# A fused attention and two-MoE kernel on one core: late weights loaded into tiles of other owners, and a re-ordered last stage

## The chip, the cores and the metric

The kernel runs on one core of one Trainium2 chip. The metric is the device time of one execution in microseconds (us), lower is better. The engines are PE (matrix products; PEld is its weight load), DVE (vector), ACT (scalar functions and copies), POOL (a second, slower vector engine) and SP, which here only issues DMAs from HBM.

## The reference

Three blocks follow each other. All inputs are float32 except the last three weight matrices, which come out of the third block's draw in float64.

```
B, H, S, D = 4, 8, 576, 64; stride = 32
scores = q @ k.T / sqrt(D)              # heads 0-3: rel in [0, 32); heads 4-7: pos equal modulo 32, causal
attn   = softmax(mask(scores)) @ v      -> x: 2304 x 512
logits = x @ phi                        # 512 x 32: 8 experts of 4 slots
slots  = softmax(logits, over tokens).T @ x          # 32 x 512
for e in 8: slot_out[e] = relu(slots[e] @ w1[e]) @ w2[e]    # 512 x 1024, 1024 x 512
x      = softmax(logits, over slots) @ slot_out
out    = (silu(x @ w_gate) * (x @ w_val)) @ w_out    # 512 x 1536 twice, 1536 x 512
```

## The kernel before, in words

**Attention stage.** Sixteen units (two batches times one head each) run in a software pipeline that one loop counts by `n`. Iteration `n` multiplies unit `n`'s queries and keys (L283) on PE, adds the mask and takes the maximum on DVE (L287, L288), transposes unit `n-1` (L300), takes exponentials on ACT (L293), and multiplies unit `n-1` by its values (L316). Keys lie in three tiles `k0` to `k2`, values in two tiles `v0` and `v1`, the masks in `ml` and `ms`; all of these lie in the pool `ld`. POOL copies each value tile once more into its lower 32 partitions (L261). Between the units stand the transposes of finished heads (L335, copied out by ACT at L337), the logits (L357) and, at the end, the softmax over tokens and the slots (L378 to L473). Lists called `side`, `mid_`, `late` and `first_` say behind which part of which iteration such a step is put.

**Expert stage.** `w1_mm` (L631) runs over the 16 halves of w1 in the order `W1ORDER`, then L722 over the 16 halves of w2 in the order `W2ORDER`. Each half is a tile of 128x2048 (1 MB), loaded as two DMAs of 512 KB.

**Loads.** SP issues every load in the order of the program text, and a load waits on SP until its tile is free; whatever stands behind it on SP waits too. `load_half` takes the next entry of a list. Fifteen weight tiles lie in pool `wp`. Before, the weights 22, 24 and 26 go to a pool `wp2` that takes the place of `ld` after the last unit, and halves of the weights 0, 13, 14 and 15 go into tiles of the attention stage (`wx`, `tmp`).

**Last stage.** The 2304 tokens form blocks `bi` of 512, 512, 512, 512 and 256; the 1536 hidden columns form 12 slices `f`. A step (`bi`, `f`) is `gv` (two products, L800 and L801, then Silu on ACT, a product on DVE, a rounded copy `hh` on ACT and the rest `hl` on POOL, L806 to L809) and, three steps (`LAG`) later, `omm` (L827: 12 products of 128x512 for a block of 512). `CUTS` says which slices of a block are summed in which of three passes; after a pass the block's four PSUM banks are evacuated by DVE and ACT (L852, L858, L862). A slice `f` can be used when its float64 weights have been turned into float32: per 1 MB tile two magnitudes on ACT (`mag`, L199), two clamps on POOL (L206), and three operations each on both halves on DVE (`shift`, `low`, `sign`: L217, L221, L225). For a gate/value tile `g` two small products follow (`a_mm` L780, `a_st` L787) that give `St`. `ORDER` is the order of these tiles, `stage` starts one, `part` issues one DVE operation when a budget (`room`) allows it. `HEAD` is the order of the first small steps; `warm` issues products with no use but to keep PE busy.

Of the kernel before, what the change touches and what calls it, by code (L numbers as in the profile page):

```python
# [32 lines left out]
WORDER = PRE[:2] + list(range(1, 13)) + list(W2ORDER[:6]) + list(SPEC) + [SPLIT] + list(W2ORDER[6:6]) + PRE[2:] + list(W2ORDER[6:])  # L33
# [3 lines left out]
ORDER = [("g", 2), ("g", 3), ("o", 1), ("g", 4), ("o", 2), ("g", 5), ("o", 3), ("g", 6), ("g", 7), ("g", 8), ("g", 9), ("o", 4), ("g", 10), ("g", 11), ("o", 5)]  # L37
LAG = 3
CVC = 0.6
CLP = "go"  # L40
WTAIL = 4
NQK = 3
# [7 lines left out]
ROOM0 = 0.1  # L50
STG = 2
ROOMS = (0.8, 1.2, 0.6)
ROOM = 2.5
EV = 1.1
DIRECT = (2,3,2)
# [58 lines left out]
def build(ctx: ExitStack, tc: tile.TileContext, cst, phi, kq, vh, w1, w2, wgv, wo, out):  # L114
# [9 lines left out]
    pp = [es_p.enter_context(tc.tile_pool(name="pp", bufs=1, space=bass.MemoryType.PSUM))]  # L124
    es_ld = ExitStack()
    lp = es_ld.enter_context(tc.tile_pool(name="ld", bufs=1, side="right"))
    es_att = ExitStack()
# [17 lines left out]
    for j in range(NV):  # L145
        vt.append(lp.tile([96, 2 * NT * (HD + 1)], F32, name=f"v{j}"))
    col = lp.tile([128, 128], F32, name="col")
    par = lp.tile([128, 16], F32, name="par")
    loc = lp.tile([128, 8], F32, name="loc")
    ml = lp.tile([128, 5, 96], BF16, name="ml")  # L150
    ms = lp.tile([128, 9, 96], BF16, name="ms")

    wsrc = [w1[j] for j in range(16)] + [w2[j] for j in range(16)]
    loads = [(j, hf) for j in WORDER for hf in range(2)]
    loads.remove((SPLIT, 0))
    loads.remove((SPEC[0], 1))
    loads.insert(2 * (NB + 2 + NB2), (SPLIT, 0))
    loads.insert(2 * (NB + 2), (SPEC[0], 1))
    wt, gt = {}, {}
    wn = [0]  # L160
    NW = len(loads)

    def load_half(k, pool=wp, bufs=NB):
        for _ in range(k):
            if wn[0] >= NW:
                return
            j, hf = loads[wn[0]]
            if j in SPEC:
                wt[j, hf] = (ap_.tile([128, 1024], F32, tag="wy" if hf else "xT", name="wx", bufs=1) if j == SPEC[0] else
                             ap_.tile([128, 1024], F32, tag="x", name="wx", bufs=6))  # L170
            elif j == SPLIT:
                wt[j, hf] = ap_.tile([128, 1024], F32, tag="eT", name="wx", bufs=1) if hf else tmp[:, 0:1024]
            elif hf == 0:
                a = pool.tile([128, 2048], F32, tag="w", name="w", bufs=bufs)
                if j in PRE:
                    gt[j] = a.bitcast(I32)
                wt[j, 0], wt[j, 1] = a[:, 0:1024], a[:, 1024:2048]
# [271 lines left out]
    def weights_b():  # L449
# [12 lines left out]
    szt = []  # L462

    szp = []

    def slot_in(st, bp):
# [4 lines left out]
        if bp:  # L471
            for y in range(2):
                DVE.tensor_copy(szt[0][:, 2 * y + st, :].rearrange("p (e k) -> p e k", k=36)[:, :, 0:4],  # L473
                                szp[0][:, 64 * st + 32 * y:64 * st + 32 * y + 32].rearrange("p (e j) -> p e j", j=4))
# [9 lines left out]
    with tc.manual_schedule():  # L484
# [39 lines left out]

        def strided():
            for i in range(NT):
# [7 lines left out]
        POOL.memset(eT, 0.0)  # L534

# [23 lines left out]
        for bp in range(2):  # L559
# [5 lines left out]
            else:  # L565
                for fn, d in ((tok_max, 1), (tok_nm, 1), (e_perm, 2), (tok_end, 2), (tok_copy, 2)):
                    at_late(b0 + d, fn, 0)
# [10 lines left out]
            else:  # L578
                at_late(b0, load_half, 4)
                at_late(b0 + 1, warm, WTAIL)  # L580
                for fn, *a in ((etr, 1, 0), (etr, 1, 1), (slot, 1, 0, 0, 3), (etr, 1, 2),
                               (slot, 1, 0, 3, 9), (load_half, 2), (slot_end, 1, 0), (slot, 1, 1, 0, 9),
                               (slot_end, 1, 1), (slot_in, 0, 0), (slot_in, 1, 0), (slot_in, 0, 1),
                               (load_half, 2), (warm, WT[0]), (slot_in, 1, 1), (warm, WT[1])):
                    at_late(b0 + 2, fn, *a)
        at_late(0, strided)
        at_late(1, sels)
        for k, n in PRECONV:
            at_late(k, pre, n)
        n = 0  # L590
        while n < 16 or any(k >= n for k in late):
# [15 lines left out]
            if 0 <= n - 1 < 16:  # L607
                pv(n - 1)
                load_v(n + 1)
                if n == 16:  # L610
                    load_half(2 * (NB + 2) + 1 - wn[0])
                    es_ld.close()
                    wp2 = es_w2.enter_context(tc.tile_pool(name="wp2", bufs=NB2, side="right",
                                                           reuse_waits="tile"))
                    load_half(2 * NB2, wp2, NB2)
                    szt.append(wp2.tile([128, 4, 288], F32, name="sz", bufs=1))
                    POOL.memset(szt[0], 0.0)
# [146 lines left out]
        acc = [fr.tile([128, 512], F32, name=f"acc{t}") for t in range(18)]  # L764

# [118 lines left out]
        def stage(n):  # L884
            if queue and len(staged) < 2:
# [112 lines left out]
```

## Time and profile before

| what | us |
|---|---|
| runs | 346.71, 348.81, 349.77 (median 348.81) |
| profiled execution, its own time | 347.91 |
| its span, first to last instruction | 346.1 |
| PE busy | 330.6 (96%) |
| DVE, ACT, POOL busy | 223.6, 192.7, 139.6 |
| DMA moved | 71.93 MB, mean 208 GB/s |

The span splits into the attention stage (0 to 105.2 us), the expert stage (105.2 to 139.9) and the last stage (from 145.2, the first L800). "Idle before" in square brackets is time in which the engine had nothing running just before that row, and what released it. Times are counted from the span's start.

### The profile page before, as it was taken

How to read it: one execution, taken by the hardware profiler on the slowest of the kernel's cores; microseconds unless marked ns; L12 is line 12 of the kernel's file. 1: busy time of each engine (PE TensorE's matmuls, PEld its weight loads, DVE VectorE, ACT ScalarE, POOL GpSimd, SP SyncE). 2: the span in 40 equal slices, each digit the busy share in tenths (PEclk: the TensorE clock that was granted, in tenths of full speed). 3: DMA queues.
4: the chain of work that ended last, by engine and by line, in shares of the span. 5: the costliest groups of instructions: out<-in, count | busy, mean ns of one | idle time of the engine just before them, and what ended most of it. 6: DMA issues, size and time to landing. Idle time of an engine off the chain costs nothing.

```text
span 346.1 us, 7436 instructions
## 1 busy us (share of the span) xinstructions
PE 330.6 (96%) x2852; PEld 246.5 (71%) x2852; DVE 223.6 (65%) x472; ACT 192.7 (56%) x460; POOL 139.6 (40%) x169
## 2 busy tenths in 40 slices
PE   8799999899999999989996999999999999999995
PEld 5588888697774433567774777777776888888884
DVE  5998888878550356477879588978886233243342
ACT  3798898886530123567567455655556344354441
POOL 2232333112300200357546549655857543443431
PEclk9999999999999999999999899999999999999999
DMA  7999999997899999823335506333000002030331
GB/s 284 411 409 407 396 400 390 407 407 270 280 377 335 411 411 399 321 101 123 128 116 151 205 16 236 122 124 121 1 2 0 0 18 105 0 121 2 123 121 61
DMA packets 20803, 71.93 MB, mean 208 GB/s; under 512 B 2336, under 2 KB 2720, under 8 KB 20768
## 3 DMA queue, kind: packets, MB, share of 16 engines
q1 hardware_dynamic: 20624, 71.45, 55.0%
q8 instruction: 22, 0.36, 0.4%
q14 instruction: 13, 0.11, 0.1%
q10 hardware_dynamic: 144, 0.01, 0.0%
HBM read 66.73 MB, written 4.72 MB: 206 GB/s over the span
## 4 chain that ended last, share of the span: by engine, by line
PE 70%; DVE 12%; DMA 8%; ACT 6%; issue 2%; POOL 1%; SPq 0%; DVEq 0%; POOLq 0%
PE o L827 35%; DMA w<-in_w 5%; PE pv L722 4%; PE sc L631 4%; PE sc L283 4%; PE pv L316 3%; PE gv L800 3%; DMA v<-in_vh 3%; PE gv L801 3%; DVE h L807 3%; PE tr L300 2%; PE tr L335 2%; DVE cv L217 2%; ACT tmp L293 1%; PE tr L482 1%
## 5 line engine op out<-in xcount | busy, mean ns | idle before, releaser
L809 POOL TENSOR_TENSOR hl<-h,hh 128x512 fp32r<-128x512 f32 (+1 forms) x60 | 72.6, 1210 | 88.5 <-ACT hh L808 88.4
L827 PE MATMUL o<-woh,hh 128*128 128x512 f32 (+1 forms) x222 | 86.8, 392 | 2.1 <-DVE acc L852 1.6
L827 PE MATMUL o<-wol,hh 128*128 128x512 f32 (+1 forms) x222 | 86.1, 390 | 0.0
L807 DVE TENSOR_TENSOR h<-gv,sg 128x512 f32<-128x512 f32 (+1 forms) x59 | 37.5, 636 | 60.9 <-ACT sg L806 48.8
L827 PE MATMUL o<-woh,hl 128*128 128x512 f32 (+1 forms) x222 | 66.2, 391 | 0.0
L808 ACT CAST hh<-h 128x512 fp32r<-128x512 f32 (+1 forms) x60 | 34.7, 578 | 52.0 <-DVE h L807 51.0
L827 PEld LDWEIGHTS o<-woh,hh 128*128 128x128 f32 x222 | 41.9, 189 | 13.4 <-DVE acc L852 2.8
L261 POOL COPY v<-v 32x390 f32<-32x390 f32 (+1 forms) x48 | 23.7, 528 | 61.9 <-DMA v<-in_vh 54.8
L827 PEld LDWEIGHTS o<-woh,hl 128*128 128x128 f32 x222 | 42.0, 191 | 9.2
L827 PEld LDWEIGHTS o<-wol,hh 128*128 128x128 f32 x222 | 42.0, 189 | 8.4
L806 ACT ACTIVATE sg<-gv 128x512 f32<-128x512 f32 (+1 forms) x60 | 33.4, 557 | 23.8 <-PE gv L800 23.3
L293 ACT ACTIVATE tmp<-tmp,mx 128x96 f32<-128x96 f32 x144 | 40.1, 368 | 9.3 <-DVE mx L288 9.3
L283 PE MATMUL sc<-k 64*64 64x96 f32 x576 | 27.7, 246 | 1.4 <-DVE tmp L287 1.1
L800 PE MATMUL gv<-cs,St 128*128 128x512 f32 (+1 forms) x60 | 25.4, 423 | 2.3 <-DVE St L789 2.0
L283 PEld LDWEIGHTS sc<-k 64*64 64x64 f32 x576 | 24.3, 133 | 4.4 <-DVE tmp L287 1.7
L771 POOL TENSOR_TENSOR wol<-wo,woh 128x512 fp32r<-128x512 f32 x12 | 15.3, 1288 | 23.8 <-ACT woh L768 23.8
L316 PEld LDWEIGHTS pv<-v,tmp 96*64 96x64 f32 x576 | 19.8, 137 | 6.1 <-ACT tmp L301 5.0
L301 ACT COPY tmp<-tr 96x384 f32<-96x384 f32 x48 | 19.6, 477 | 7.8 <-PE tr L300 7.7
L316 PE MATMUL pv<-v,tmp 96*64 96x65 f32 x576 | 22.3, 226 | 1.4 <-ACT tmp L301 1.1
L801 PE MATMUL gv<-cs,St 128*128 128x512 f32 (+1 forms) x59 | 22.3, 377 | 0.5 <-DVE h L807 0.4
L300 PE MATMUL tr<-cst_t,tmp 128*96 128x128 f32 x144 | 20.0, 280 | 1.5 <-ACT xT L337 1.5
L221 DVE SCALAR_TENSOR_TENSOR cv<-g,cv 128x512 int32<-128x512 int32 x30 | 20.8, 694 | 0.8
(161 smaller groups left out, 460.3 us busy)
## 6 DMA issues: line engine op xcount, KB each, us to landing
w<-in_w SPq DMA_DIRECT2D x56, 512.0 KB, 8.1
g<-in_wgv SPq DMA_DIRECT2D x10, 1024.0 KB, 5.0
k<-in_kq SPq DMA_DIRECT2D x16, 576.0 KB, 7.7
g<-in_wo SPq DMA_DIRECT2D x5, 1024.0 KB, 4.9
v<-in_vh SPq DMA_DIRECT2D x16, 292.5 KB, 6.2
out<-osb SPq DMA_DIRECT2D x17, 256.0 KB, 2.1
wx<-in_w SPq DMA_DIRECT2D x7, 512.0 KB, 5.3
w<-in_wgv SPq DMA_DIRECT2D x4, 512.0 KB, 7.8
```

The source lines that it names most:

```text
L261: POOL.tensor_copy(t4[0:W - 64, :, i0:i1, :], t4[64:W, :, i0 - 1:i1 - 1, :])
L283: PE.matmul(out=ps[h, W * (i - i0):W * (i - i0) + W], lhsT=q[h, 64 * i:64 * i + 64], rhs=k[h, c0:c0 + W], start=True, stop=True, skip_grou ...
L293: ACT.activation(out=e[:, i], in_=e[:, i], func=AF.Exp, scale=1.0, bias=mx[:, i:i + 1])
L300: PE.transpose(ps[0:W, 128 * j:128 * j + 128], e[:, 3 * t + j], ident)
L316: PE.matmul(out=ps[64 * b:64 * b + 64, 65 * (i - i0):65 * (i - i0) + 65], lhsT=attile[0:W, i, 64 * b:64 * b + 64], rhs=v[0:W, 65 * (NT * b ...
L800: PE.matmul(out=pg[:, 0:n], lhsT=St[f][:, 0:128], rhs=csf[:, t0:t0 + n], start=True, stop=True)
L801: PE.matmul(out=pvv[:, 0:n], lhsT=St[f][:, 128:256], rhs=csf[:, t0:t0 + n], start=True, stop=True)
L806: ACT.activation(out=sg[:, 0:n], in_=pg[:, 0:n], func=AF.Silu)
L807: DVE.tensor_tensor(out=h[:, 0:n], in0=pvv[:, 0:n], in1=sg[:, 0:n], op=ALU.mult)
L808: ACT.copy(hh[bi, f][:, 0:n], h[:, 0:n])
L809: POOL.tensor_tensor(out=hl[bi, f][:, 0:n], in0=h[:, 0:n], in1=hh[bi, f][:, 0:n].bitcast(F32), op=ALU.subtract)
L827: PE.matmul(out=o[:, 0:c], lhsT=(a, a, l)[i][:, 128 * t:128 * t + 128], rhs=(woh, wol, woh)[i][f][:, c * k:c * k + c], start=(first and i ...
```

## The change

1. **Homes.** The pools `wp2` and the closing of `ld` are gone. `HOME` names, half tile by half tile, a tile that the attention stage has finished with: key and value tiles, the mask tile, `tmp`, `eT`, `xT` and the six `x` tiles. `LOADS` is a written list of all loads, and `WSCHED` and some `at_step`/`at_late` say when each is issued. `W1ORDER` changes so that the weights in attention tiles (`ATT`) are used by the eleventh place.
2. **Masks.** All masks lie in one tile `mt`. Six of the nine strided masks are computed before the first unit, three after it. The clearing of `eT` on POOL moves from the start to iteration 3.
3. **Copies.** The three copies L337 of one head pair (1,0,0) go from ACT to DVE; in iteration 11 they come ahead of the other late steps, and the copy `Lb` ahead of `e_perm`. One `warm` product less at the end of the attention stage (`WTAIL`).
4. **Last stage.** `CUTS`: block 0's second pass has slices 1 to 3 (was 1 to 4), block 4's has slice 3 alone (was 3 to 5). `ORDER` converts g5 and g6 ahead of o2. `STG` 1 (was 2), `ROOM` 2.4 (was 2.5). `HEAD` puts a transpose (`t`) ahead of `a0` and both `s` steps ahead of the `warm` products. The order of the first eight `acc` tiles and the `g` buffers in memory changes.
5. **Clamps.** `DC=(0,0,2)` files the two clamps of a staged tile under step `n+0`, whose list has already been run when `stage(n)` files them. The built program has no clamp on POOL at all (29 before). The clamps matter only for weights outside float32's range.

```diff
-NB2 = 3
-SPEC = (0, 14, 15)
-SPLIT = 13
-WORDER = PRE[:2] + list(range(1, 13)) + list(W2ORDER[:6]) + list(SPEC) + [SPLIT] + ...
+HOME = {(0, 1): "wy", (0, 0): "xT", (11, 0): "tmp1", (13, 0): "tmp0", (13, 1): "eT",
+        (14, 0): "x", (14, 1): "x", (15, 0): "x", (15, 1): "x", (12, 0): "x", (12, 1): "x",
+        (26, 0): "k1", (26, 1): "k2", (28, 0): "k0", (28, 1): "mt", (11, 1): "v0", (30, 0): "v1"}
+LOADS = (both(*PRE[:2], *range(1, 11), 16, 18, 20, 22) + [(26, 0), (26, 1)] + both(24) +
+         [(0, 1), (28, 0), (28, 1), (11, 1), (13, 0), (30, 0), (0, 0), (11, 0)] + both(14, 15) +
+         [(13, 1), (12, 0), (12, 1)] + both(PRE[2]) + [(30, 1)] + both(*range(17, 32, 2)))
-W1ORDER = (1, 2, 3, 4, 5, 6, 0, 7, 14, 8, 15, 9, 10, 13, 12, 11)
+W1ORDER = (1, 2, 3, 4, 0, 14, 5, 15, 6, 13, 12, 11, 8, 10, 7, 9)
-ORDER = [("g", 2), ("g", 3), ("o", 1), ("g", 4), ("o", 2), ("g", 5), ("o", 3), ("g", 6), ("g", 7), ("g", 8), ...
+ORDER = [('g', 2), ('g', 3), ('o', 1), ('g', 4), ('g', 5), ('g', 6), ('o', 2), ('g', 7), ('o', 3), ('g', 9), ...
+MSC = 6
+TC = 2
+FST = (11,)
+ETM = 3
+DC = (0, 0, 2)
+XTD = {(1,1,1):(0,1),(1,0,0):(0,1,2)}
-WTAIL = 4
+WTAIL = 3
-STG = 2
+STG = 1
-ROOM = 2.5
+ROOM = 2.4
-HEAD = "h g a0 t a1 t s0 w1 s1 p1 w1"
+HEAD = 'h g t a0 a1 t s0 s1 w1 p1 w1 w1'
-WHEAD = 5
-WSCHED = [2]*12+[4,4,2,0,0]
+WHEAD = 4
+WSCHED = [2]*12+[2,2,2,2,0]
-CUTS = [(0, 1, 5, 12), (0, 2, 6, 12), (0, 2, 7, 12), (0, 3, 8, 12), (0, 3, 6, 12)]
+CUTS = ((0, 1, 4, 12), (0, 2, 6, 12), (0, 2, 7, 12), (0, 3, 8, 12), (0, 3, 4, 12))
...
-        cp_ = DVE.tensor_copy if (bp, y, st) == (1, 1, 1) and t in (0, 1) else ACT.copy
+        cp_ = DVE.tensor_copy if t in XTD.get((bp, y, st), ()) else ACT.copy
...
+        strided(0, MSC)
+        at_late(0, strided, MSC, NT)
+        at_late(ETM, POOL.memset, eT, 0.0)
+        at_step(13, load_half, 1)
+        at_late(14, load_half, 3)
+        at_step(15, load_half, 3)
+        at_late(15, load_half, 1)
...
-                    load_half(2 * (NB + 2) + 1 - wn[0])
-                    es_ld.close()
-                    wp2 = es_w2.enter_context(tc.tile_pool(name="wp2", bufs=NB2, side="right", ...
-                    load_half(2 * NB2, wp2, NB2)
+                    load_half(2)
...
-            for fn, a in late.pop(n, []) + first_.pop(n, []):
+            last_, f_ = late.pop(n, []), first_.pop(n, [])
+            for fn, a in f_ + last_ if n in FST else last_ + f_:
...
-                        at(n + 1 + k, fn, k)
-                staged.append((n + 2, kind, j, parts[z:]))
+                        at(n + DC[k], fn, k)
+                staged.append((n + DC[2], kind, j, parts[z:]))
```

**SP at the end of the attention stage.** `w` is a weight tile of `wp` (or, before, of `wp2`), `wx` a weight in an attention tile. Before:

```order
L258 DMA v1_80<-in_vh 64x1170
L182 DMA w_1354<-in_w2 128x1024 x2
L258 DMA v0_79<-in_vh 64x1170
L258 DMA v1_80<-in_vh 64x1170
L182 DMA wx_1676<-in_w1 128x1024
L182 DMA w_1682<-in_w2 128x1024 x2
L182 DMA w_1685<-in_w2 128x1024 x2
L182 DMA w_1688<-in_w2 128x1024 x2
L182 DMA tmp_86<-in_w1 128x1024
```

Now:

```order
L204 DMA w_1345<-in_w2 128x1024 x2
L204 DMA w_1393<-in_w2 128x1024
L280 DMA v0_79<-in_vh 64x1170
L204 DMA w_1393<-in_w2 128x1024
L204 DMA k1_77<-in_w2 128x1024
L280 DMA v1_80<-in_vh 64x1170
L204 DMA k2_78<-in_w2 128x1024
L204 DMA w_1555<-in_w2 128x1024 x2
L204 DMA wx_1603<-in_w1 128x1024
L204 DMA k0_76<-in_w2 128x1024
L204 DMA mt_81<-in_w2 128x1024
```

The value loads of the last units no longer stand behind the pair that waits for the second preloaded tile's conversion (w_1354, now w_1555), and the loads into key, mask and value tiles stand between and behind them.

**ACT at the start of the last stage**, from the second step's Silu (`sg`) to the first evacuation. Before:

```order
L806 ACTIVATE sg_2294<-gv_2290 128x512
L808 CAST hh_2296<-h_2295 128x512
L806 ACTIVATE sg_2315<-gv_2311 128x512
L808 CAST hh_2317<-h_2316 128x512
L199 ACTIVATE wg3_2168<-g_2172 128x512 x2
L852 COPY acc2_2216<-o_2332 128x512
```

Now:

```order
L827 ACTIVATE sg_2284<-gv_2280 128x512
L829 CAST hh_2286<-h_2285 128x512
L221 ACTIVATE wg3_2157<-g_2169 128x512 x2
L827 ACTIVATE sg_2306<-gv_2302 128x512
L829 CAST hh_2308<-h_2307 128x512
L873 COPY acc2_2161<-o_2321 128x512
```

The two magnitudes stand ahead of the third step's Silu instead of behind its `hh`.

**DVE where block 4's first pass ends** (`acc16` evacuates its bank; `h` is a step's product). Before:

```order
L807 TENSOR_TENSOR h_2660<-gv_2656,sg_2659 128x512
L225 SCALAR_TENSOR_TENSOR wo0_60<-g_2360,cv_2643 128x512
L217 TENSOR_SCALAR cv_2668<-wo0_60 128x512
L221 SCALAR_TENSOR_TENSOR cv_2668<-g_2360,cv_2668 128x512
L852 COPY acc16_2230<-o_2619 128x512
L807 TENSOR_TENSOR h_2692<-gv_2688,sg_2691 128x512
L225 SCALAR_TENSOR_TENSOR wo0_60<-g_2360,cv_2668 128x512
L217 TENSOR_SCALAR cv_2705<-wg1_59 128x512
L221 SCALAR_TENSOR_TENSOR cv_2705<-g_2438,cv_2705 128x512
L225 SCALAR_TENSOR_TENSOR wg1_59<-g_2438,cv_2705 128x512
L789 TENSOR_TENSOR St4_2182<-gv_2727,St4_2182 64x256
```

Now:

```order
L828 TENSOR_TENSOR h_2650<-gv_2646,sg_2649 128x512
L243 SCALAR_TENSOR_TENSOR cv_2630<-g_2348,cv_2630 128x512
L247 SCALAR_TENSOR_TENSOR wg1_59<-g_2348,cv_2630 128x512
L239 TENSOR_SCALAR cv_2661<-wg2_2156 128x512
L873 COPY acc16_2219<-o_2606 128x512
L810 TENSOR_TENSOR St4_2179<-gv_2673,St4_2179 64x256
L828 TENSOR_TENSOR h_2682<-gv_2678,sg_2681 128x512
```

`St4` now stands right behind `acc16`; before, six other operations stood between. The operations on `wo0` (the o2 tile) have left this place, those on `wg1` (g5) are nearly done here.

## Rows read from the trace of the kernel before

**Rows 1.** The profile page, part 2, PE's busy tenths in 40 slices.

```profile
PE   8799999899999999989996999999999999999995
```

**Rows 2.** Busy by stretch: PE, PEld, DVE, ACT, POOL; then PEclk, DMA share, GB/s.

```profile
17.50:53.00 35.50, 35.26 (x647) 30.31 (x644) 31.02 (x79) 32.25 (x104) 11.09 (x21) 1.00 1.02 401
...
70.00:88.00 18.00, 17.57 (x320) 15.07 (x316) 14.06 (x35) 14.06 (x47) 5.07 (x12) 1.00 0.90 325
88.00:105.20 17.20, 16.48 (x217) 12.74 (x216) 9.85 (x39) 6.86 (x21) 1.51 (x2) 1.00 0.91 344
105.20:120.90 15.70, 15.36 (x138) 7.55 (x137) 2.76 (x10) 2.05 (x3) 2.02 (x1) 1.00 0.97 371
120.90:139.90 19.00, 19.00 (x158) 6.67 (x159) 11.38 (x30) 5.22 (x8) 0.00 (x0) 1.00 1.00 396
...
175.00:200.50 25.50, 22.25 (x98) 16.12 (x97) 20.29 (x33) 14.56 (x30) 15.23 (x17) 0.93 0.42 141
200.50:264.00 63.50, 62.95 (x303) 47.40 (x301) 54.54 (x88) 37.45 (x73) 40.09 (x41) 1.00 0.26 84
```

**Rows 3.** Timeline of the start: time, us, engine, line, operation [idle before <-releaser].

```profile
5.67 0.66 DVE L287 SCALAR_TENSOR_TENSOR tmp<-sc,ml 128x480 f32<-128x480 f32 x1 [2.21 <-PE sc L283]
...
7.98 3.83 DVE L509 TENSOR_SCALAR ms<-cst_t,par 128x96 bf16<-128x96 f32 x9
...
19.45 1.50 POOL L261 COPY v<-v 32x260 f32<-32x260 f32 x3 [7.76 <-DMA v<-in_vh]
```

**Rows 4.** Timeline, PE's transposes of unit 11.

```profile
65.88 1.30 PE L300 MATMUL tr<-cst_t,tmp 128*96 128x128 f32 x9 [1.54 <-ACT xT L337]
```

**Rows 5.** Groups by line, DVE copies of xT: busy us, mean ns, idle before.

```profile
L337 DVE COPY tmp<-tr 128x384 f32<-128x384 f32 x2 | 1.0, 552 | 0.4 <-ACT xT L337 0.4
```

**Rows 6.** Waits of SP's queue: us in total, times, longest us.

```profile
SPq L182 <- DVE wg L225: 7.8, 1, 7.8
```

**Rows 7.** Timeline, PE: the value products of units 12 and 13.

```profile
75.34 1.22 PE L316 MATMUL pv<-v,tmp 96*64 96x65 f32 x36
...
81.00 1.89 PE L316 MATMUL pv<-v,tmp 96*64 96x65 f32 x36
```

**Rows 8.** Timeline, PE: warm products, first w2 half, head of the last stage.

```profile
96.17 1.04 PE L482 MATMUL tr<-warm_t 128*128 128x512 bf16 x4
...
120.89 1.34 PE L722 MATMUL pv<-w,hz 128*32 128x512 f32 x8 [0.34 <-DVE hz L709]
...
141.84 0.64 PE L780 MATMUL gv<-wg,soT 128*32 128x256 f32 x8 [0.38 <-DVE soT L748]
```

**Rows 9.** Timeline, PE's waits in the last stage.

```profile
152.38 0.50 PE L827 MATMUL o<-woh,hh 128*128 128x512 f32 x1 [0.90 <-DVE acc L852]
...
184.20 0.50 PE L801 MATMUL gv<-cs,St 128*128 128x512 f32 x1 [0.45 <-DVE h L807]
...
186.84 0.50 PE L827 MATMUL o<-woh,hh 128*128 128x512 f32 x1 [0.75 <-DVE acc L852]
...
190.99 0.50 PE L800 MATMUL gv<-cs,St 128*128 128x512 f32 x1 [2.05 <-DVE St L789]
...
263.65 0.50 PE L827 MATMUL o<-woh,hh 128*128 128x512 f32 x1 [0.49 <-DVE acc L858]
```

**Rows 10.** Timeline, ACT: magnitudes ahead of an evacuation.

```profile
151.69 1.23 ACT L199 ACTIVATE wg<-g 128x512 f32<-128x512 f32 x2
```

**Rows 11.** Timeline, DVE: the evacuation at block 4's first pass.

```profile
186.10 0.68 DVE L852 COPY acc<-o 128x512 f32<-128x512 f32 x1
```

**Rows 12.** Chain of waits: twelve output products after the 2.05 us wait, and later.

```profile
191.72 4.35 PE o L827 x12
...
269.52 2.76 PE o L827 x12
```

**Rows 13.** Groups by line, POOL's clamps.

```profile
L206 POOL TENSOR_SCALAR wg<-wg 128x512 f32<-128x512 f32 x19 | 11.7, 618 | 0.0
L206 POOL TENSOR_SCALAR wo<-wo 128x512 f32<-128x512 f32 x10 | 6.2, 615 | 0.0
```

More of the change, by code (lines that the diff above doesn't have):

```diff
@@ L124, in build @@
     pp = [es_p.enter_context(tc.tile_pool(name="pp", bufs=1, space=bass.MemoryType.PSUM))]
-    es_ld = ExitStack()
-    lp = es_ld.enter_context(tc.tile_pool(name="ld", bufs=1, side="right"))
+    lp = es_w2.enter_context(tc.tile_pool(name="ld", bufs=1, side="right"))
     es_att = ExitStack()
@@ L145, in build @@
     for j in range(NV):
[L146 to L151, printed above, removed]
-    wsrc = [w1[j] for j in range(16)] + [w2[j] for j in range(16)]
-    loads = [(j, hf) for j in WORDER for hf in range(2)]
-    loads.remove((SPLIT, 0))
-    loads.remove((SPEC[0], 1))
@@ L157, in build @@
-    loads.insert(2 * (NB + 2 + NB2), (SPLIT, 0))
-    loads.insert(2 * (NB + 2), (SPEC[0], 1))
+        vt.append(lp.tile([128, 2 * NT * (HD + 1)], F32, name=f"v{j}"))
+    mt = lp.tile([128, 1024], F32, name="mt")
+    col, par, loc = mt[:, 0:128], mt[:, 128:144], mt[:, 144:152]
+    ml = mt[:, 152:392].bitcast(BF16).rearrange("p (j k) -> p j k", k=W)
+    ms = mt[:, 392:824].bitcast(BF16).rearrange("p (j k) -> p j k", k=W)
+    sz = lp.tile([128, 4 * 256 + 32], F32, name="sz")
+    wsrc = [w1[j] for j in range(16)] + [w2[j] for j in range(16)]
@@ L159, in build, with place @@
     wt, gt = {}, {}
     wn = [0]
-    NW = len(loads)
-    def load_half(k, pool=wp, bufs=NB):
+    def place(j, hf):
+        h = HOME.get((j, hf))
+        if h is None:
+            if (j, 1 - hf) in wt and (j, 1 - hf) not in HOME:
+                return
+            a = wp.tile([128, 2048], F32, tag="w", name="w", bufs=NB)
+            if j in PRE:
+                gt[j] = a.bitcast(I32)
+            for k in range(2):
+                if (j, k) not in HOME:
+                    wt[j, k] = a[:, 1024 * k:1024 * k + 1024]
+        elif h[0] in "kv":
+            wt[j, hf] = (kt if h[0] == "k" else vt)[int(h[1])][:, 0:1024]
+        elif h == "mt":
+            wt[j, hf] = mt
+        elif h[:3] == "tmp":
+            o = (0, 1728)[int(h[3])]
+            wt[j, hf] = tmp[:, o:o + 1024]
+        else:
+            wt[j, hf] = ap_.tile([128, 1024], F32, tag=h, name="wx", bufs=6 if h == "x" else 1)
@@ L164, in load_half @@
+    def load_half(k):
         for _ in range(k):
-            if wn[0] >= NW:
+            if wn[0] >= len(LOADS):
                 return
[L167 to L177, printed above, removed]
+            j, hf = LOADS[wn[0]]
+            place(j, hf)
@@ L472, in slot_in @@
             for y in range(2):
-                DVE.tensor_copy(szt[0][:, 2 * y + st, :].rearrange("p (e k) -> p e k", k=36)[:, :, 0:4],
+                DVE.tensor_copy(sz[:, 512 * y + 256 * st:512 * y + 256 * st + 288].rearrange("p (e k) -> p e k", k=36)[:, :, 0:4],
                                 szp[0][:, 64 * st + 32 * y:64 * st + 32 * y + 32].rearrange("p (e j) -> p e j", j=4))
@@ L523, in build, with strided @@
         same(ident, 0, 128, loc)
-        def strided():
-            for i in range(NT):
+        def strided(a, b):
+            for i in range(a, b):
                 cut(ms[:, i], 6 + i, ALU.is_lt, h)
@@ L532, in sels @@
             same(selt, 2, 64)
-        POOL.memset(eT, 0.0)
         side, late, mid_, first_ = {}, {}, {}, {}
@@ L565, in build @@
             else:
-                for fn, d in ((tok_max, 1), (tok_nm, 1), (e_perm, 2), (tok_end, 2), (tok_copy, 2)):
+                for fn, d in ((tok_max, 1), (tok_nm, 1), (tok_copy, TC), (e_perm, 2), (tok_end, 2)):
                     at_late(b0 + d, fn, 0)
@@ L583, in build @@
                                (slot_end, 1, 1), (slot_in, 0, 0), (slot_in, 1, 0), (slot_in, 0, 1),
-                               (load_half, 2), (warm, WT[0]), (slot_in, 1, 1), (warm, WT[1])):
+                               (load_half, 3), (warm, WT[0]), (slot_in, 1, 1), (warm, WT[1])):
                     at_late(b0 + 2, fn, *a)
-        at_late(0, strided)
+        strided(0, MSC)
+        at_late(0, strided, MSC, NT)
+        at_late(ETM, POOL.memset, eT, 0.0)
         at_late(1, sels)
+        at_step(13, load_half, 1)
+        at_late(14, load_half, 3)
+        at_step(15, load_half, 3)
+        at_late(15, load_half, 1)
         for k, n in PRECONV:
@@ L610, in build @@
                 if n == 16:
[L611 to L617 removed]
+                    load_half(2)
+                    POOL.memset(sz, 0.0)
             if n < 11:
                 load_half(WSCHED[n + 1])
[L620 removed]
+            last_, f_ = late.pop(n, []), first_.pop(n, [])
+            for fn, a in f_ + last_ if n in FST else last_ + f_:
                 fn(*a)
@@ L630, in w1_mm @@
             for c in (0, 2, 1, 3):
-                PE.matmul(out=hps[hf][32 * c:32 * c + 32, :], lhsT=szt[0][:, c, 32 * e:32 * e + 32],
+                PE.matmul(out=hps[hf][32 * c:32 * c + 32, :], lhsT=sz[:, 256 * c + 32 * e:256 * c + 32 * e + 32],
                           rhs=wch(j, c), start=(j == first[hf]), stop=(j == last[hf]), skip_group_check=True)
-            if j not in SPEC and j != SPLIT:
+            if j not in ATT:
                 load_half(2)
@@ L640, in build @@
         rest = list(W1ORDER)
-        while any(j in rest for j in SPEC + (SPLIT,)):
+        while any(j in rest for j in ATT):
             w1_mm(rest.pop(0))
@@ L758, in build @@
         wos.append(fl.tile([128, 1024], F32, name="wo1"))
+        acc = [fr.tile([128, 512], F32, name=f"acc{t}") for t in range(8)]
         for _ in range(NG):
@@ L763, in build @@
         wol = [fr.tile([128, 512], F32R, name=f"wol{f}") for f in range(12)]
-        acc = [fr.tile([128, 512], F32, name=f"acc{t}") for t in range(18)]
+        acc += [fr.tile([128, 512], F32, name=f"acc{t}") for t in range(8, 18)]
         def split_hi(j):
```

23 lines of the change are left out of this document (13 added, 10 removed).

## The prediction

> **What bounds the kernel now.** I read the page's busy slices first: PE shows 8 or 9 in every slice [rows 1], and it is busy for 330.6 of 346.1 us. So a change can only win where PE stands still or where its products run slowly, and the 15.5 us of idle, with what a lower clock takes, are the most there is. The second view, the stretches [rows 2], says where the rest lies. From 17.5 to 53 PE is full and the DMA moves 401 GB/s with a share of 1.02: the loads have no gap. From 70 to 120.9 the rate falls to 325, 344 and 371 GB/s, so loads wait there, while PE is nearly full. In the w2 products (120.9 to 139.9) both PE (19.00 of 19.00) and DMA (396 GB/s) are full, side by side. Then comes the place with the largest loss: from 175 to 200.5 PE is busy 22.25 of 25.50 us and its granted clock is 0.93, the only one of the seven stretches under 1.00. From 200.5 to 264 PE waits for 0.55 us only, with DVE busy 54.54 of 63.50. The third view is the timeline, read at the gaps.
>
> **The sum** is made against the profiled execution's own 347.91 us, 0.9 below the median of 348.81. A measurement of this kernel can tell a difference of about 1%, so "faster" means under 345.3 and "slower" over 352.3.
>
> **Masks.** Nine strided masks took 3.83 us, 0.426 each, between the first unit's maxima and the next unit [rows 3]. Six of them, 2.6 us, now run ahead of the first addition of a mask, which stood at 5.67 after 2.21 us in which DVE waited. How much of the 2.6 fits into those 2.21 us hangs on when the mask numbers land, which no row shows: unit 0 is later by 0.4 to 2.6 us, and I take half of the masks, 1.3. Units 1 and 2 come earlier by the other half, 1.3, because only three masks are left behind unit 0. What holds the gain back: unit 2's values were copied by POOL from 19.45 to 20.95 after a load [rows 3], and that load is not moved. Bounds: a loss of 1.3 (the late start stays) and a gain of 1.3. I take 0.7, nearer to the gain, since PE is full again from 17.5 [rows 2].
>
> **Copies.** PE waits 1.54 us at 64 for an ACT copy that had stood behind exponentials [rows 4]. On DVE three such copies cost 3 x 0.552 = 1.7 us [rows 5], and that is time by which the next unit's mask addition on DVE comes later. Bounds 0 and 1.54; I take 0.4, near the lower end, because the row after the gap waits on DVE next.
>
> **Value loads.** SP waited once for 7.8 us, for the conversion of a preloaded weight, with the values of units 13 and 14 queued behind it [rows 6]. Unit 13's value products took 1.89 us, unit 12's 1.22 [rows 7]: 0.67 of late data. In the new order both value loads stand ahead of that wait. Gain 0.65, bounds 0 and 0.67.
>
> **Smaller edits of the first part.** One of four `warm` products goes, 1.04/4 = 0.26 [rows 8], and the work behind it does not wait: 0.25 (bounds 0 and 0.26). PE's 0.34 before the first w2 half [rows 8] is covered, because a w1 half that was ahead of the hidden layer now stands behind it: 0.4 with the weight load that follows (bounds 0 and 0.4). The move of the clearing of `eT` costs nothing: POOL is idle for 7.76 us at 11.7 to 19.45 [rows 3] and has 11.09 busy of the next 35.50 [rows 2]. Together the first part gives 0.7 + 0.4 + 0.65 + 0.25 + 0.4 = **2.4 us**.
>
> **The cover that this needs.** w2 runs at the pace of its loads, so a PE that arrives 2.4 us earlier would only wait, unless the loads come earlier too. The homes let SP issue them while the attention stage ends. The gaps there, against 401 GB/s, are (18 x 76 + 17.2 x 57 + 15.7 x 30) / 401 = 7.0 us of transfer [rows 2]. I estimate that about 4 of them are closed: the homes come free one by one and SP still waits at some. 4 is more than 2.4, so I charge nothing.
>
> **Head of the last stage.** A transpose moves into the 0.38 us in which PE waits for `soT` [rows 8]: 0.4 (bounds 0 and 0.5).
>
> **Waits of the last stage.** Five rows [rows 9] sum to 0.90 + 0.45 + 0.75 + 2.05 + 0.49 = 4.64 us.
> (a) At 152.38 PE waits 0.90 for an evacuation. Two magnitudes, 1.23 us on ACT [rows 10], now stand ahead of the third step's Silu; `h`, `hh` and the evacuation behind it come later by up to that. I take a loss of 1.2 (bounds 0 and 1.23).
> (b) 0.45 and 2.05 go. Both come from slice 4, which the second pass needed as its last. With the cut at 4 it is needed two steps later, and a step takes 2.76 + 0.46 = 3.2 us [rows 12], so 6.4 us later. On DVE, six operations of 0.69 on o2, 4.1 us, have left the place between `acc16` and `St4`. Gain 2.5, bounds 0 and 2.5.
> (c) The 0.75 before block 4's evacuation stays. Ahead of `acc16` there are still a product and three conversions, and PE arrives there earlier by the waits that went. DVE is busy 20.29 of 25.50 us [rows 2], so it has little room. I take a loss of 1.45, so a wait of 2.2 (bounds: a gain of 0.75, a loss of 2.5).
> (d) Right after the wait of 2.05 us, twelve output products took 4.35 us, and 2.76 elsewhere [rows 12]: 1.6 us of granted clock at the lower of its two levels, 1.2 GHz, for some of the products. If no wait of that length follows on an idle gap, the 1.6 returns. The gap of 1.54 at 64 was not followed by such a fall. I give it back, with bounds 0 and 1.6.
> (e) The 0.49 at 263.65 is half filled by the later o tiles: 0.25.
> Net 2.5 - 1.2 - 1.45 + 1.6 + 0.25 = **1.7 us**.
>
> **Clamps.** 11.7 + 6.2 = 17.9 us of POOL go [rows 13]. POOL's work is on the path at none of PE's five waits, so I count nothing. They could also pull DVE's conversions forward; that lies within (c)'s bounds.
>
> **Other slices and cuts.** The number of products is the same; only their order differs. DVE's evacuations keep their number and their 0.68 us each [rows 11].
>
> 347.91 - 2.4 - 0.4 - 1.7 = **343.4 us**. Its own range, from the terms' bounds, is 341 to 346.
>
> **Rivals.**
> *All waits of the last stage go.* If DVE runs ahead because the clamps and o2 are out of its way, then (a), (c) and (e) vanish too. All 4.64 and the 1.6 come back: 347.91 - 2.4 - 0.4 - 6.2 = 338.9. For it: 20% of DVE's time from 175 to 200.5 is idle [rows 2]. Against it: the magnitudes ahead of the Silu are certain. Chance 0.17.
> *The clock falls again.* If the wait at (c) takes the place of the one at `St4` and is as long, the 1.6 is lost again: 345.0. For it: my own 2.2 in (c) is longer than 2.05. Against it: it would have to be one gap and not two. Chance 0.17. [...]
> *The loads are no earlier.* There is one SP queue. If each home's release makes it wait again, the gaps from 70 to 120.9 stay, the last w2 half lands when it did, and PE waits in w2 for the 2.4 it had won: 347.91 - 0.4 - 1.7 = 345.8. For it: a single wait already took 7.8 us [rows 6]. Chance 0.10. The Trainium skill (DMA: Bandwidth & Descriptors, "Anatomy of one DMA — SWDGE (gpsimd) path") says that DMA engines don't wait on semaphores and the wait is on the issuing sequencer; the trace agrees with its 7.8 us wait of SP.
> *The change does nothing.* Every gain is taken back by the next wait: 347.9. Chance 0.08.
> *Slower: DVE never catches up.* From 200.5 to 264 a step of 3.2 us holds 54.54 / (63.5 / 3.2) = 2.75 us of DVE work, 0.45 of slack, less than one operation of 0.69. Slices come one step earlier for the second passes and `room` is smaller, so a lag is worked off slowly. If the lag passes one step (3.2 us), PE waits about 2.05 at each of the ends of blocks 1 to 3, and each such wait is followed by 1.6 of slow products: 343.4 + 3 x 3.65 = 354.3. Against it: PE lost only 0.55 in that stretch. Chance 0.08.
>
> **How the numbers follow.** The forecast has 0.40. Faster by over 1%: nine tenths of the forecast (0.36), the 0.17 of 338.9 and 0.09 of the clock's 0.17, together 0.62. Within 1%: 0.04 + 0.08 + 0.10 + 0.08 = 0.30. Slower: 0.08. The range is 338.5 to 347.5; it takes in four cases and leaves out the slower one and about half of "nothing".
>
> **What would show it.** Right: unit 2's value products starting about 0.7 earlier; no 1.54 gap at 64; unit 13's value products at 1.2; rates near 400 GB/s from 70 to 120.9; the first L800 about 2.8 earlier; no wait before `St4`; a wait of about 2 before `acc2` and `acc16`, and the clock at 1.00 from 175 to 200. Wrong: a PE gap on w2's DMA; a wait of over 2 us followed by slow products; DVE named at the ends of blocks 1 to 3.

## The result

| | us, median (lowest to highest) | runs |
|---|---|---|
| before | 349.29 (346.71 to 350.37) | 4 |
| after | 343.01 (342.31 to 345.55) | 4 |
| ratio after/before | 0.9848, 95% interval 0.9801 to 0.9895 | |

The kernel became 1.5% faster. The forecast was 343.4 us with a range of 338.5 to 347.5; the time is right, but it was reached by terms of which several were wrong in size and one edit, (a), was wrong in its net sign. That the sum still came within 0.4 us is in part luck, as the section on the prediction shows.

The profiled execution of after is the slowest of its four: 345.55, span 343.8. Its page shows why, and so does a second profiled execution of the same kernel, from the first experiment (343.82, span 341.7). Part 2 of the page, after:

```profile
PE   8979999999999999989998999999999999999995
PEclk9989999999999999998999999999999999999999
```

The row PEclk of the second profile has a 9 in every slice. The 7 in PE's third slice is a wait for unit 2's values (below). The two 8s of PEclk are stretches at the lower granted clock. Busy time by stretch of the first profile, columns as in [rows 2]:

```profile
20.00:25.00 5.00, 4.87 (x63) 4.18 (x61) 2.04 (x7) 2.62 (x8) 1.68 (x5) 0.66 1.02 406
...
154.00:158.00 4.00, 4.00 (x13) 3.10 (x12) 2.68 (x4) 1.98 (x4) 1.29 (x1) 0.59 0.35 73
```

and of the second:

```profile
20.00:25.00 5.00, 4.70 (x83) 4.07 (x84) 2.73 (x9) 3.44 (x12) 1.49 (x4) 1.00 1.02 408
...
154.00:158.00 4.00, 4.00 (x19) 3.29 (x18) 3.63 (x6) 2.61 (x5) 1.30 (x1) 1.00 0.34 106
```

From 154 to 158 PE is as busy in both (4.00 of 4.00), but does 13 products in one and 19 in the other. From here on the second profile stands for after where lengths are compared; a stage that holds a fall of the clock is marked *.

| stage, by the first PE instruction of the next | before | after, first profile | after, second |
|---|---|---|---|
| attention, to w1 | 105.17 | 106.03* | 105.66 |
| w1 and hidden layer, to w2 | 15.72 | 15.33 | 15.34 |
| w2, to the first `a_mm` | 20.95 | 20.65 | 20.65 |
| head, to the first L800 (now L821) | 3.38 | 2.85 | 2.85 |
| last stage, to the end | 200.90* | 198.90* | 197.21 |

So the last stage gives 3.7 us, of which 1.6 is the clock's [rows 12], and the w1, w2 and head stages 0.4 + 0.3 + 0.5. These four lengths repeat within 0.1 us in the profiles below, wherever the program of the stage and the clock are the same.

The attention stage does not repeat like that. The second profile is in its turn the slowest execution of its four (343.82; the others took 342.89 to 343.17), and its 105.66 is the longest of six profiles of this same attention program without a fall in that stage: mag_late and cut5 end it at 104.48, stg2 at 104.56, clamps at 105.13, first_only at 105.61. The program of before ended it at 105.17 and, in last_only, at 106.07. So this stage, which was to give 2.0 of the 2.4, gives somewhere between a loss of half a microsecond and a gain of one and a half, and no single pair of profiles tells which. From unit 10's value products to w1 the profiles agree better: 44.99 and 45.27 with the program of before, 44.46 to 44.50 with the changed one.

These are the rows of the second profile that answer to [rows 9], PE's timeline:

```profile
150.56 0.50 PE L822 MATMUL gv<-cs,St 128*128 128x512 f32 x1 [0.23 <-ACT sg L827]
152.47 0.51 PE L848 MATMUL o<-woh,hh 128*128 128x512 f32 x1 [1.42 <-ACT acc L873]
...
184.51 0.50 PE L822 MATMUL gv<-cs,St 128*128 128x512 f32 x1 [0.81 <-DVE h L828]
...
186.77 0.51 PE L848 MATMUL o<-woh,hh 128*128 128x512 f32 x1 [0.82 <-ACT acc L873]
```

No wait for `St4`, none at 263. In the last stage the waits sum to 3.28 instead of 4.64. In the attention stage, in answer to [rows 3, 4, 7], the first profile's wait for unit 2's values, then (second profile) the place at 64, what follows it, and unit 13:

```profile
19.80 2.47 PE L338 MATMUL pv<-v,tmp 96*64 96x65 f32 x36 [1.77 <-DMA v<-in_vh]
```

```profile
65.40 1.43 PE L322 MATMUL tr<-cst_t,tmp 128*96 128x128 f32 x9
67.25 0.69 PE L379 MATMUL lg<-xT,phi_t 128*32 128x288 f32 x8 [0.42 <-DVE Lb L418]
...
72.86 0.53 PE L322 MATMUL tr<-cst_t,tmp 128*96 128x128 f32 x3 [0.47 <-ACT eT L443]
73.63 1.03 PE L322 MATMUL tr<-cst_t,tmp 128*96 128x128 f32 x6 [0.24 <-ACT eT L443]
...
82.31 1.27 PE L338 MATMUL pv<-v,tmp 96*64 96x65 f32 x36
```

The wait of 1.54 is gone and three others have come, 1.13 together; unit 13's value products take 1.27 instead of 1.89. In answer to [rows 2], the second profile's stretches of loads:

```profile
70.00:88.00 18.00, 17.29 (x325) 14.79 (x321) 15.15 (x38) 14.80 (x50) 4.88 (x11) 1.00 0.88 308
88.00:105.00 17.00, 16.56 (x211) 12.37 (x209) 9.49 (x37) 7.53 (x24) 1.46 (x3) 1.00 1.02 405
105.00:121.00 16.00, 15.70 (x139) 7.97 (x143) 4.08 (x13) 1.56 (x2) 2.02 (x1) 1.00 1.02 408
```

The gaps from 88 to 121 are closed (344 and 371 GB/s before), the one from 70 to 88 has grown (325 before, 308 now).

### The profile page after: what moved, and what is told of

The parts are those of the page before. It is cut to its first block, busy times and chain, and to the rows that moved or that the text cites. A ratio compares the mean times of both kernels' runs of the same rounds, so it can differ in the third digit from the quotient of the medians.

```text
span 343.8 us, 7397 instructions
## 1 busy us (share of the span) xinstructions
PE 330.6 (96%) x2857; PEld 248.2 (72%) x2857; DVE 226.3 (66%) x475; ACT 192.8 (56%) x457; POOL 121.4 (35%) x140
## 4 chain that ended last, share of the span: by engine, by line
PE 81%; ACT 7%; DVE 5%; DMA 4%; issue 2%; DVEq 0%; SPq 0%; POOL 0%; POOLq 0%
PE o L848 42%; PE pv L742 4%; PE pv L338 4%; PE sc L651 4%; PE sc L305 4%; PE gv L821 4%; PE tr L322 3%; PE gv L822 3%; ACT tmp L315 3%; DMA v<-in_vh 2%; PE tr L357 2%; PE gv L801 2%; DMA k<-in_kq 2%; PE lg L379 1%; PE gv L808 1%
## 5 line engine op out<-in xcount | busy, mean ns | idle before, releaser
L283 POOL COPY v<-v 32x390 f32<-32x390 f32 (+1 forms) x48 | 22.6, 503 | 63.4 <-DMA v<-in_vh 47.6
L821 PE MATMUL gv<-cs,St 128*128 128x512 f32 (+1 forms) x60 | 25.6, 426 | 0.0
L322 PE MATMUL tr<-cst_t,tmp 128*96 128x128 f32 x144 | 21.0, 281 | 1.0 <-ACT eT L443 0.7
```

The lines of the kernel that those rows point to most:

```text
L283: POOL.tensor_copy(t4[0:W - 64, :, i0:i1, :], t4[64:W, :, i0 - 1:i1 - 1, :])
L322: PE.transpose(ps[0:W, 128 * j:128 * j + 128], e[:, 3 * t + j], ident)
L821: PE.matmul(out=pg[:, 0:n], lhsT=St[f][:, 0:128], rhs=csf[:, t0:t0 + n], start=True, stop=True)
```

## Experiments

Every ratio is to runs of the kernel before on the same chip. In the first four runs after itself stood at 343.04. The others ran on other chips, where before took 348.47 to 348.84 instead of 348.12, so a difference of less than about 0.7 us between medians of different chips tells nothing; there the lengths of stages decide.

**again.** No edit.

> The changed kernel once more, unaltered. Its profiled execution took 345.55 us while the other three took 342.3 to 343.3; its trace has two stretches at the lower clock, 20 to 25 us (right after a 1.77 us wait for unit 2's values) and 154 to 157 us (right after a 1.42 us wait for acc2), worth about 3.5 us together. Theory (the falls come in some executions only, and then right after these waits): median 343, a spread of 3 us, and a profile with falls at these two places or at none of them. Rival (falls have nothing to do with waits): falls at other places.

Measured: 343.04 (342.89 to 343.82), ratio 0.9865 (0.9845 to 0.9886). Mean granted clock 1.00 in all four runs, and no fall in the profile, though the wait of 1.42 stands there as before and unit 2's values were waited for 0.98 us. The theory holds as far as these two profiles go: falls followed such waits in one execution and not in the other.

**first_only and last_only.** The change in two halves.

```diff
 first_only: change, but CUTS, ORDER, STG, ROOM, HEAD, WHEAD of before
-DC = (0, 0, 2)
+DC = (1, 2, 2)
 last_only: before, but CUTS, ORDER, STG, ROOM, HEAD, WHEAD of the change
-                        at(n + 1 + k, fn, k)
+                        at(n, fn, k)
```

> Homes, masks and copies of the change, with the last stage of before (its slices per pass, order of conversion, head, room, and the clamps). Theory of the prediction (both parts give, 2.4 of the first and 2.1 of the last): 2 to 3 us under before, ratio 0.992 to 0.994. Rival (the first part is eaten by its own new wait at unit 2's values and the fall of the clock behind it): within 0.5 us of before, ratio 0.998 to 1.002.

> The kernel before with only the last stage of the change (slices per pass, order of conversion, head, room, staging one step earlier, no clamps). Theory of the prediction: 2.1 us under before, ratio 0.994. Rival (all of the gain is here): 5 us under before, ratio 0.985.

Measured: first_only 346.35, ratio 0.9946 (0.9918 to 0.9973); last_only 345.59, ratio 0.9931 (0.9907 to 0.9954). At 348.12 for before that is 1.9 and 2.4 us, against the predicted 2.4 (first_only has the old head) and 2.1 (last_only has the new one): both parts give, and 0.9946 x 0.9931 = 0.9877 is nearly the whole. Both rivals fall. The one profile of first_only is the slowest of its twelve executions (348.74): it shows w1 and w2 0.7 us shorter, as in after, an attention stage 0.4 longer and a fall of the clock behind the 2.05 us wait. Where the rest of its 1.9 lies, it doesn't show. last_only has the loads of before. There PEld's idle time that ended with the landing of a w2 half was 1.5 us (0.5 in before), w2 took 21.85 us instead of 20.95, and this although PE began w2 0.9 later than in before: the loads of before have no time to spare. In after no such wait is left.

**masks_old.**

```diff
-MSC = 6
+MSC = 0
```

> The changed kernel with all nine strided masks computed after unit 0 again. The prediction: 0.7 us slower than the changed kernel. Rival (the early masks only move the wait to unit 2's values, where a 1.77 us wait opens and the clock falls): the changed kernel loses nothing, it gains up to 1 us, and no fall between 20 and 25 us.

Measured: 343.36 (342.95 to 344.81), ratio 0.9885 (0.9863 to 0.9908), beside 343.04 with early masks: no difference that can be told. The attention stage ends at 104.36 with the old masks, just below the 104.48 to 105.66 of the early ones. The prediction's 0.7 is not there.

**v2_first, v2_spread.** What holds the early masks back?

```diff
-WSCHED = [2]*12+[2,2,2,2,0]
+WSCHED = [2,0,4]+[2]*9+[2,2,2,2,0]       (v2_first)
+WSCHED = [2,0]+[2]*10+[4,2,2,2,0]        (v2_spread)
```

> The changed kernel with the second pair of weight loads issued behind unit 2's values instead of ahead of them. Theory (early masks are worth nothing because unit 2's values come too late, a wait of 1.0 to 1.8 us): that wait goes, the attention stage ends 1 to 1.3 us earlier than the 105.7 of the changed kernel's second profile, median about 342. Rival (behind that wait PE's own issue gaps of 0.55, 0.19 and 0.48 us, or the next keys and values, take the time): the wait goes and the stage still ends at 105.5 or later, median 343.

Measured: 343.51, ratio 0.9861 (0.9828 to 0.9893). Unit 2's values are in time, unit 4 would start 1.8 us ahead of before, and then PE stands, in PE's and POOL's timeline:

```profile
26.87 1.94 PE L338 MATMUL pv<-v,tmp 96*64 96x65 f32 x36 [1.78 <-ACT tmp L315]
```

```profile
26.88 1.31 POOL L283 COPY v<-v 32x260 f32<-32x260 f32 x3 [8.21 <-DMA v<-in_vh]
```

PE's releaser reads as ACT, but PE and POOL start within 0.01 us, and POOL waited for the DMA of unit 3's values: the wait has moved one unit on, because four loads now stood ahead of them. The stage ended at 106.22, as the rival had it.

> The changed kernel with two weight loads fewer among the first units (none behind unit 0, so the values of units 2 and 3 each stand behind 1 MB less) and two more ahead of unit 11. In the earlier try with all four behind unit 2's values, unit 3's scores started 1.8 us ahead of before, and unit 3's values then took it all in a wait of 1.78. Theory (early masks are held back by the loads queued ahead of the values alone): unit 4 and all behind it start 1 to 1.8 us earlier than before, the attention stage ends at about 103, median 341.5. Rival (the DMA is full up to 53 us, so some later keys or values are late instead): the lead is lost by unit 7 again, stage end 104.3 to 105.5, median 343.

Measured: 341.90 (340.77 to 343.20), ratio 0.9807 (0.9767 to 0.9846). PE's busy time and the loads, in the profile:

```profile
17.50:53.00 35.50, 35.50 (x641) 30.56 (x637) 31.82 (x77) 31.96 (x101) 13.94 (x24) 1.00 1.02 402
```

PE has no gap left, the scores of units 4 to 11 start 2.0 us ahead of before, and the stage ends at 102.61, with the DMA as full as in [rows 2]; combo, with the same attention program, ends it at 103.41. That is 1.1 to 3.1 us earlier than the same masks with the change's order of loads, and 1.1 us by the medians. So the order of loads on SP took the lead of the early masks. The old masks with this new order were not run; since masks_old has no wait of PE for a load in this stage, the order alone had none to remove there, but that is argued and not measured.

**copies_act.**

```diff
-XTD = {(1,1,1):(0,1),(1,0,0):(0,1,2)}
+XTD = {(1,1,1):(0,1)}
```

> The changed kernel with the three copies of one head pair on ACT again. The prediction: 0.4 slower, 343.4, with the 1.54 us wait back at about 64. Rival (what the copies win at 64, 0.85 us in the profile, is lost again to DVE and ACT work at 67 to 74): the wait is back and the attention stage ends no later than with the copies on DVE, median 343.0 or under.

Measured: 343.69 (342.31 to 344.31), ratio 0.9853 (0.9815 to 0.9892). A wait of 1.44 is back at 65, those at 67 and 73 are gone. From unit 10's values to w1, PE needs 44.45 us with the copies on ACT (59.89 to 104.34) and 44.48 on DVE (61.18 to 105.66). The other profiles with these copies on DVE give 44.46 to 44.50, so this holds to a few hundredths: nothing won, as the rival said. (Its median is higher, but a fall of the clock stands in its profile, in the last stage.)

**clamps.**

```diff
-DC = (0, 0, 2)
+DC = (1, 2, 2)
```

> The changed kernel with its 29 clamps on POOL again. The prediction (POOL is on no wait's path): same as the changed kernel, 343.0, within 0.5. Rival (conversions on DVE wait for clamps, as in before's 1.53 us of DVE idle ahead of a product): waits for POOL on DVE, the waits at acc2 and acc16 grow, 1 to 2 us slower.

Measured: 343.65 (343.00 to 345.06), ratio 0.9867 (0.9834 to 0.9901); last stage 197.25 against 197.21. 17.9 us of POOL work weigh nothing here.

**stg2, mag_late.**

```diff
-STG = 1
+STG = 2
 mag_late, besides:
-                staged.append((n + DC[2], kind, j, parts[z:]))
+                staged.append((n + (1 if n == STG else DC[2]), kind, j, parts[z:]))
```

> The changed kernel with staging from the third step on again, so that the two magnitudes stand behind the third step's Silu. Theory (the wait for acc2 of 1.42 + 0.23 us comes from the magnitudes): that wait falls to about 0.9, 0.7 less; if nothing later takes it, median 342.3. Rival (the step by which conversions start later is missed at acc16, about 35 us behind): the waits there grow by as much or more, median 343 to 344.

> The changed kernel with only the first two magnitudes placed behind the third step's Silu again, and every DVE operation where it is in the changed kernel (so no conversion starts a step later). Theory (the growth of the wait for acc2 from 0.90 to 1.42 + 0.23 is those two magnitudes on ACT, and the 1.7 us that later staging cost came from the later conversions): the wait falls to about 0.9, nothing later grows, last stage 196.5 instead of 197.2, median 342.3. Rival (DVE now waits for the magnitudes ahead of the evacuation): the wait for acc2 stays at 1.4 or more, with DVE named, median 343 to 344.

Measured: stg2 344.27 (343.97 to 344.86), ratio 0.9881 (0.9849 to 0.9913), last stage 198.88: 1.7 longer. mag_late 341.60 (341.35 to 342.90), ratio 0.9802 (0.9766 to 0.9838), last stage 196.24: 1.0 shorter. PE's wait at `acc2`, in stg2 and then in mag_late:

```profile
150.32 0.50 PE L848 MATMUL o<-woh,hh 128*128 128x512 f32 x1 [0.86 <-DVE acc L873]
```

```profile
150.24 0.50 PE L848 MATMUL o<-woh,hh 128*128 128x512 f32 x1 [0.86 <-DVE acc L873]
```

The wait falls to 0.86 in both, so the two magnitudes ahead of the third Silu cause its growth. In stg2 the later conversions are paid for behind it, above all in a wait of 1.1 us for `wol` (POOL) at 204; in mag_late DVE's order is that of the change, and nothing grows. Earlier staging is thus a net gain of 1.7 us with a loss of 1.0 inside it.

**cut5.**

```diff
-CUTS = ((0, 1, 4, 12), ...
+CUTS = ((0, 1, 5, 12), ...
```

> The changed kernel with slices 1 to 4 in block 0's second pass again (slice 4 needed two steps earlier). The prediction (half of the 2.05 us wait before St4 came from the cut, half from o2 ahead of g5): a wait for St4 of 0.5 to 2 us is back, and the clock falls behind it in some executions, 0.5 to 2.5 us slower, 343.5 to 345.5. Rival (o2's move alone took the wait away): no wait for St4, 343.0.

Measured: 346.67 (345.38 to 348.14), ratio 0.9936 (0.9912 to 0.9960). PE's waits by releaser:

```profile
PE o L848 <- POOL wol L792: 0.9, 1, 0.9
...
PE o L848 <- ACT osb L883: 0.6, 1, 0.6
```

Neither side had it right. There is no wait for `St4`, so it was not the cut that took it away. Left are the other edits of the last stage, o2's move and the staging one step earlier above all, and no run parts these two. And yet the kernel is slower, by 3.6 us of the medians and 2.5 of the ratios: slice 4 now needs o2's weights at 199 us, and they are not there (0.9), and at 218 PE waits once more (0.6). About 1.6 more is a fall of the clock behind the 1.42 us wait, which after has in some executions too. The rest of its longer last stage (201.59 against 197.21) is not located. The cut is thus needed beside the new order of conversion.

**combo.** v2_spread and mag_late together.

> Both edits that won by themselves: two weight loads moved from behind unit 0 to ahead of unit 11, and the first two magnitudes behind the third step's Silu. They touch the attention stage and the last stage. Theory (they add up): each took 1.1 to 1.4 us off the changed kernel's 343.0, so 340.5, ratio 0.975, about 3 us under the changed kernel. Rival (the earlier arrival of PE in the last stage, or w2's loads, takes part of it): 341.5 or more.

Measured: 339.99 (339.77 to 341.24), ratio 0.9764 (0.9738 to 0.9789). They add up: 3.0 us under after, faster than both kernels. The longest waits of PE that are left are 1.1 us at the very start and 0.8 to 0.9 each at `acc2`, at `acc16` and for a step's product `h`.

## Why the prediction was right, and where it was wrong

- **The sum**: 343.4 against 343.01, in part by luck. Masks and copies, counted at 1.1 together, gave nothing, and the last stage, counted at 1.7, gave 3.7 in an execution without a fall of the clock. Its range of 341 to 346 is not what the bounds of the terms give: added up, they reach from 338 to 353. (And [rows 1] show a 7 in the second slice and a 5 in the last, not 8 or 9 in every one.)
- **The two halves**: predicted 2.4 for the first part and 0.4 + 1.7 for head and last stage, measured 1.9 (first_only) and 2.4 (last_only). Right in size; the parts inside moved against each other.
- **Masks** (0.7): wrong. Unit 0 was not late (its mask addition starts at 5.50 and 5.79 in the two profiles, [rows 3] have 5.67), since the six masks took 1.17 us there, not 2.6. The lead was 2.4 us at unit 1's values; behind unit 2's values 0.25 of it was left. PE's timeline at these two places, before and then the second profile of after:

```profile
16.56 1.40 PE L316 MATMUL pv<-v,tmp 96*64 96x65 f32 x36 [0.60 <-ACT tmp L301]
...
20.96 1.41 PE L316 MATMUL pv<-v,tmp 96*64 96x65 f32 x36 [0.24 <-ACT tmp L301]
```

```profile
14.18 1.40 PE L338 MATMUL pv<-v,tmp 96*64 96x65 f32 x36
...
20.17 1.94 PE L338 MATMUL pv<-v,tmp 96*64 96x65 f32 x36 [0.98 <-DMA v<-in_vh]
```

The prediction named that load as the brake and sized it at half of the gain; it took nearly all.
- **Copies** (0.4): the wait at 64 went and 1.13 us of waits came behind it, 0.0 by copies_act. The value was too high. The reason given for a low one, DVE's own time, fits 0.42 of these waits, for `Lb` on DVE; the other 0.71 name `eT` on ACT.
- **Value loads** (0.65): 1.89 - 1.27 = 0.62. The wait of SP for DVE's `wg` of 7.8 us [rows 6] is gone from SP's list.
- **Warm product and `hz`** (0.25 + 0.4): the stage from w1 to w2 is 0.38 shorter, as predicted for `hz`. The warm product was not tried alone; PE's next wait behind it, 0.24 for `eT`, is 0.24 in both kernels, so nothing took its place there.
- **Cover**: 4 us of load gaps were to close; those of 88 to 121 did, (17.2 x 57 + 15.7 x 30)/401 = 3.6, but the one of 70 to 88 grew by 18 x 17/401 = 0.8. It was enough: in v2_spread PE begins w2 2.95 us ahead of before, and w2 takes 20.65 us there as in after. The rival of loads that come no earlier fell with first_only.
- **Head** (0.4): 0.5.
- **Last stage, (a)** (loss of 1.2): 1.42 + 0.23 against 0.90, a loss of 0.75 in waits and of 1.0 by mag_late. The mechanism was right. What (a) failed to count is the other side of the same edit: conversions start a step earlier, worth 1.7 net by stg2.
- **(b)** (gain of 2.5): the 2.05 went, the 0.45 became 0.81, and it is 0.81 in cut5 as well, so it did not come from slice 4. The credit was put down wrongly: the new order with its earlier staging removed the wait, the cut only made that order affordable (cut5). The reading of DVE's order was wrong too: between `acc16` and `St4` stood five operations, not six, and of them one on o2, three on g5 and one product.
- **(c)** (loss of 1.45): 0.75 became 0.82. Too dark: PE was to get there earlier by the waits that went, but of those the 2.05 stood behind this place (190.99 against 186.84 us) and the 0.45 did not go. PE came 0.14 earlier, and DVE's evacuation started 0.32 later (186.42 instead of 186.10).
- **(d)** (1.6 of clock): returned in the second profile, and in part of the executions only. By the mean granted clock of each run, 8 of 17 runs of before (those beside again) lay at 0.995 or less, and 1 of 8 of after.
- **(e)** (0.25): the 0.49 went whole.
- **Clamps** (nothing): right.
- **The rival of the clock** was half right: its wait of over 2 us did not come, but a fall came after one of 1.42 in the first profile.

Left open: in the second profile PE has three gaps of 0.55, 0.19 and 0.48 us at 16 to 33 us with no releaser shown ("issue"). Such gaps stand at these places in first_only, copies_act, stg2, mag_late, cut5, combo and clamps too (there the first is 1.37), and in none of before, last_only, masks_old, v2_first, v2_spread and the first profile of after. They are part of why the attention stage does not repeat; no run here tells their cause.

## What to carry to other kernels

A wait that an edit removes is worth what the next resource leaves of it: before pricing earlier work, read when the next inputs land, and in which order the one load queue issues them. Where two edits belong together (a tile converted later, and the slice that needs it moved later), price them as one, since one without the other can lose. An edit that starts a chain earlier on one engine can be kept while the one operation that it pushes ahead of a critical one is put back; here that split was worth 1.0 us. And a stage that does not repeat between executions of one program can't be priced from one profile of each kernel: here the attention stage of one program differed by 1.2 us.

## What the runs showed of the hardware

After some waits of PE the granted clock fell to the lower of its two levels, 1.2 GHz: in two of two profiles after 2.05 us (before, first_only), in three of nine after 1.42 us at `acc2` (after, copies_act, cut5), in none of three after 0.85 or 0.86 there (stg2, mag_late, combo). The runs' mean clocks agree: of the 55 runs of the kernels with the 1.42 us wait 28 lie at 0.995 or less, of the 16 runs of the three with 0.86 none. Length alone does not decide it. In the attention stage the clock fell after 1.77 us in after, but not after 1.78 in v2_first, 1.71 in last_only, 1.54 in before and 1.44 in copies_act; what else counts, no run here shows.

A mask on DVE costs 0.2 us on average in one place and twice as much in another. The masks ahead of unit 0 in after (DVE's timeline):

```profile
4.42 1.17 DVE L529 TENSOR_SCALAR mt<-cst_t,mt 128x96 bf16<-128x96 f32 x6 [0.97 <-DMA mt<-in_cst]
```

The nine behind unit 0 in masks_old:

```profile
8.80 2.68 DVE L529 TENSOR_SCALAR mt<-cst_t,mt 128x96 bf16<-128x96 f32 x9
```

They took 3.83 in before [rows 3], from 7.98 to 11.81, and not evenly. By duration in ns (shortest, median, longest) the masks of before, and then all eleven of masks_old:

```profile
L509 DVE TENSOR_SCALAR ms<-cst_t,par x9: 257/259/2318, 8.0 to 9.8; 128x96 bf16<-128x96 f32 x9
```

```profile
L529 DVE TENSOR_SCALAR mt<-cst_t,mt x11: 257/270/564, 2.7 to 10.9; 128x96 bf16<-128x96 f32 x10, 128x384 bf16<-128x384 f32 x1
```

One mask of before took 2.3 us. POOL's timeline of before at that time:

```profile
9.37 1.33 POOL L261 COPY v<-v 32x260 f32<-32x260 f32 x3 [0.98 <-DMA v<-in_vh]
10.65 1.05 POOL L534 MEMSET eT<- 128x1152 f32 x1
```

POOL has nothing to do in the 3 us ahead of 7.54 in after, and copies beside some of the masks of masks_old (7.84 to 9.14 and 10.02 to 11.42); in before the clearing of `eT` stands there as well, and the last mask ends 0.1 us after it. That DVE is held up while POOL works fits all these rows and was not tried alone. It would make the moved clearing, which the prediction priced at nothing, worth up to 1.15 us of DVE at that place (3.83 - 2.68).
